# Windowed attention feeding a leaky-ReLU MLP: a new order of the first loads, batch 1 on five banks, and softmax sums over paired halves

## The chip, the cores and the metric

The kernel runs on one core of a Trainium2 chip. The metric is the device time of one execution in microseconds (us), measured around the whole program; the kernel before takes 304.47 us (median of 3 runs, 304.13 to 305.33).

## The reference, cut to what matters

```python
# q, k, v: (8 batches, 8 heads, 576 tokens, 64), float32
scores = q @ k.T / 8
# heads 0-3 (plain):   token i sees j with 0 <= i - j < 32
# heads 4-7 (dilated): token i sees j with 0 <= i - j < 128 and (i - j) % 4 == 0
attn = exp(scores - max) ;  attn /= sum(attn)
x = (attn @ v), heads side by side        # (4608 tokens, 512)
h = x @ w_in                              # w_in (512, 2048)
out = maximum(0.01 * h, h) @ w_out        # w_out (2048, 512), out (4608, 512)
```

## The kernel before, in words

**Attention.** A batch is worked in four *visits* of two heads each, in the order 2, 3, 0, 1: visits 2 and 3 are the dilated heads (group g = 1), visits 0 and 1 the plain ones (g = 0). Keys are cut into nine steps of 64; a visit has two *units* of 288 queries (`unit`, L685). A unit is a chain over all engines: TensorE makes the scores in a PSUM bank (L732), ScalarE takes the exponential into a tile `ee` (L739), VectorE multiplies with a 0/1 mask table (L743, batches 2 to 7; in batches 0 and 1 TensorE adds a bias instead, L728), TensorE sums the exponentials over keys by a matmul with a block of ones (L754, `z`) and multiplies with V (L756, both print as L750), ScalarE turns the sum into its reciprocal by Ln and Exp (L761, L763), and VectorE writes the normalised result as float16 into `xt` (L774). In a plain unit the score matmuls of 96 columns overlap: a query of the second half of a step's 96 columns meets the next step's first 32, so that 416 columns of `ee` fold into 288 sums.

**Getting there.** For batches 2 to 7 the planner's DMAs fetch rows of 128 bytes, GpSimd casts them to float16 (L373), and VectorE transposes 32x32 blocks (L585, L590, L597). Batches 0 and 1 (`EARLY`) are fetched in longer rows: the first 512 tokens of q and k in rows of 1 KB (`load_qk`, L429), the last 64 tokens apart (`load_rest`, L475), and TensorE turns them: four transposes at a time for the long part (`turn`, L620), eight for the last tokens (`turn_rest`, L661), both by way of one bank, `tp`. The turned pieces go on into the operand slots by copies on VectorE and ScalarE (L384, L386). `turn_rest` stands behind the second visit's `turn` (L1074 to L1076). V of the early dilated visits (`load_v` with g = 1, L510 to L516) comes in six DMAs, each into 64 partitions.

**MLP.** Tokens are cut into twelve chunks of 384. `up` (L784) multiplies a chunk with w_in, 16 blocks j of 128 hidden rows, four visits each (L793), and ScalarE applies the leaky ReLU into `gt` (L808). Chunk 1 straddles batches 0 and 1 and is done in two halves of 192 columns with one activation per block and half. Chunks 9 to 11 go through `up_seven` (L1157), a form with seven products instead of eight. The first four token tiles of 128 go through `down` (L820): 16 matmuls of 512 columns with w_out (L832), in parts of four blocks; the other 32 tiles in eight groups of four (`group`, L872, matmuls L922), which also need sums of w_out made by VectorE (L862).

**Order.** Nothing is ordered by hand but the first loads. `FIRST` (L29) lists them: w0 to w7 are w_in in pieces of 0.5 MB, w8 to w15 w_out, `qbg` is q and k of batch b, group g (1.05 MB; `q01` is batch 0, dilated), `rb` the last 64 tokens of batch b (0.26 MB), `vbg` the values (0.59 MB), `c` the mask table (0.4 MB); a dot gives one more place to a value load that comes in pieces. All go to SyncE's DMA queue in that order (two of `q01` and the identity matrix go by ScalarE's). Everything else is a task with engines to choose from, an assumed duration (such as the costs in `cast`, L366, and `move`, L387), a latency and its dependences; `_Plan.forward` (L93) simulates the engines, multiplying durations by `MARGIN` once the planned time is past `CALM` (L22, L27), `backward` gives new priorities, and the best of nine passes fixes the instruction order of every engine. An engine works strictly in that order. Filler matmuls (L1301) fill planned TensorE gaps at the start.

**Banks.** PSUM has eight banks: `tp` for turning, `sps`, `ops` x2 for attention, `hps` x2 for `up`, `fps` x2 for `down`. A bank is passed on in the order in which tasks are created (`grab`, L341). Batch 0 also uses `fps[0]` and `hps[1]` (L1078); batch 1 has three banks (L1080).

Of the kernel before, what the change touches and what calls it, by code (L numbers as in the profile page):

```python
# [18 lines left out]
RAMP = 0  # L19
# [7 lines left out]
def _margin(name, at):  # L27
    return MARGIN[name] if at > CALM else 1.0
FIRST = ('w0 q01 r0 v01 . q00 . . . . w1 v00 . w2 w3 w4 w5 w6 w7 q11 r1 q10 v11 w8 w9 . '  # L29
         'w10 v10 . . . w11 . w12 . w13 . c . w14 w15')  # L30


def _constants():
# [5 lines left out]
    last = []  # L39
# [5 lines left out]
    plain1 = [band] * 3 + [band[:, :64], band[:, 32:]]  # L45
# [204 lines left out]
def kernel(  # L250
# [54 lines left out]
    vst = [sbuf(f"vst{i}", [128, 1152], FP32) for i in range(NVS)]  # L305
    slots = sbuf("slots", [128, NT * TS])
    turned = [sbuf(f"turned{i}", [128, 640]) for i in range(NX)]
    ee = [sbuf(f"ee{i}", [128, 512]) for i in range(NE)]
# [56 lines left out]
    def cast(dst, src, n, deps, prio, engines=("POOL", "DVE"), slow=1.0):  # L365
        cost = {"POOL": (0.05 + n * 0.00102) * slow, "DVE": 0.07 + n * (0.00055 if slow == 1.0 else 0.0011),  # L366
                "ACT": (0.06 + n * 0.00087) * slow}

        def fn(e):
            if e == "ACT":  # L370
                nc.scalar.copy(out=dst, in_=src)
            else:
                ENG[e].tensor_copy(out=dst, in_=src)  # L373
        return add(tuple((e, cost[e]) for e in engines), None, 0.2, deps, fn, prio, 0.0, "cast")
# [5 lines left out]
    def move(dst, src, n, deps, prio, eng=("DVE",), dense=False):  # L380

        def fn(e):
            if e == "ACT":
                nc.scalar.copy(out=dst, in_=src)  # L384
            else:
                ENG[e].tensor_copy(out=dst, in_=src)  # L386
        cost = {"DVE": 0.11 + n * (0.00062 if dense else 0.001), "ACT": 0.08 + n * 0.00095,  # L387
                "POOL": 0.07 + n * 0.0011}
# [100 lines left out]
    def load_v(b, g, prio, at_step=None):  # L489
# [5 lines left out]
        def when(x):  # L495
            n[0] += 1
            return at_step[n[0] - 1] if at_step else prio + x
        for hh in range(2):
# [76 lines left out]
    def turn(b, vi, prio):  # L575
# [5 lines left out]
        if b >= EARLY:  # L581
# [4 lines left out]
            if dil:  # L586
# [4 lines left out]
                q_ready[b, vi] = [add("POOL", 0.72, 0.2, [tq] + old, lambda e: nc.gpsimd.tensor_copy(  # L591
# [63 lines left out]
    def turn_rest(b, prio):  # L655
        c, r_users = raw[b, "rest"]
        t_old, t_users = grab(tpb)

        def pe(e):
            for i in range(8):  # L660
                nc.tensor.transpose(tpb[:, i * 64:i * 64 + 64], rest[0:64, i * 128:i * 128 + 128],  # L661
                                    ident[0:64, 0:64])
        tt = add("PE", 0.23, 0.25, c + [t_id] + t_old, pe, prio, 0.2)
        r_users.append(tt)
        for g in (1, 0):
# [3 lines left out]
            if g:  # L669
                dst = slot(t0, 128, 0, 128, [TS, 2], [144, 4], [1, 16])  # L670
                src = at(tpb, 0, 128, g * 128, [64, 2], [1, 4], [4, 16])
            else:
                dst = slot(t0, 512, 0, 128, [TS, 2], [1, D])
                src = at(tpb, 0, 128, g * 128, [64, 2], [1, D])
            mq = move(dst, src, 128, [tt] + old, prio, ("DVE", "ACT"))
            mk = [move(slot(t0, KB + 1024 + 64 * hh, 64 * hh, 64 * hh + 64, [TS, 2], [1, D]),
                       at(tpb, 64 * hh, 64 * hh + 64, 256 + g * 128, [64, 2], [1, D]), 128,
                       [tt] + old, prio, ("DVE", "ACT")) for hh in range(2)]
# [4 lines left out]
    bank_at = [0]  # L683

    def unit(b, vi, u, prio, banks):  # L685
# [25 lines left out]
        elif u == 0:  # L711
# [3 lines left out]
            bias = [(0, 384, 0, [[0, 4], [1, 96]]), (384, 32, 0, [[1, 32]])]  # L715
        else:
            n = 416
            steps = [(s, [[1, 96]], 64 * s, 96 * (s - 5), 96, 64 * s - 288, [[1, 96]]) for s in (5, 6, 7)]
            steps.append((8, [[1, 64]], 512, 288, 64, 224, [[1, 64]]))
            steps.append((4, [[1, 64]], 288, 352, 64, 0, [[1, 64]]))  # L720
            bias = [(0, 288, 0, [[0, 3], [1, 96]]), (288, 64, 0, [[1, 64]]), (352, 64, 32, [[1, 64]])]
# [32 lines left out]
        t_sum_ = add("PE", 0.188, 0.25, [t_m, t_e, t_id], second(p_bank, lambda s: block_ones),  # L754
                     prio, 0.4, "z")
# [28 lines left out]
    def up(c, j, x, n, batches, acc, ht, by_block):  # L784
# [28 lines left out]
        acc[j].append((t_a, x, n))  # L813

# [57 lines left out]
    def group(four, acts, at_time, split):  # L872
# [33 lines left out]
        def add_up(dst, a, b, op, deps, who, t_late=0.0):  # L906
            t = add("DVE", 0.63 if n_g > 3 else 0.78, 0.2, deps,
# [139 lines left out]
    for i, step in enumerate(steps):  # L1047
        if step[0] == "v":
            rows[step] = [clock[0] + 1 + i]
            waiting += [step] * {"v01": 5, "v11": 5, "v00": 1, "v10": 3}[step]  # L1050
        elif step == ".":
            rows[waiting.pop(0)].append(clock[0] + 1 + i)
# [14 lines left out]
    def attend(b, first, step):  # L1067
# [20 lines left out]
    def ups(c, x, n, batches):  # L1088
        for j in range(NJ):
# [5 lines left out]
    U_SEVEN = (9, 10, 11)  # L1095
    HF, HT = DFF // 2, 192
# [60 lines left out]
    def up_seven(c, j0, batches, ts, acc, banks, when):  # L1157
# [70 lines left out]
        p7 = product(w_sum_of(3), x_sum_of(3), "Z", True, [s_t[3], ts[3][2]], 3)  # L1228
# [15 lines left out]
    def last_seven():  # L1244
# [8 lines left out]
        for order, c in enumerate(U_SEVEN):  # L1253
            batches = [[c // 3 * 2], [c // 3 * 2, c // 3 * 2 + 1], [c // 3 * 2 + 1]][c % 3]
            ts = x_sums(c, batches, order)
            for n in range(4):
                banks = [ready.pop(0) for _ in range(3)]
                up_seven(c, 2 * n, batches, ts, all_acts[c], banks, begins[c] + 2.5 * n)
                ready += before + [banks[1]]
                before = [banks[0], banks[2]]  # L1260

    n_g = 0
    for m in range(B // 2):
# [4 lines left out]
        if 3 * m not in U_SEVEN:  # L1268
            ups(3 * m, 0, 384, [e])
        if m == 0:  # L1270
# [6 lines left out]
        else:  # L1277
            attend(o, WHEN[o], 6.5)
            if 3 * m + 1 not in U_SEVEN:
                ups(3 * m + 1, 0, 384, [e, o])  # L1280
        if 3 * m + 2 not in U_SEVEN:
# [10 lines left out]
        while n_g < len(groups) and all(all_acts[c][0] for c, _ in groups[n_g]):  # L1292
            four = groups[n_g]
            group(four, all_acts, begins[four[-1][0] + 1] + four[-1][1] * 2.0, n_g == len(groups) - 1)
            n_g += 1
# [56 lines left out]
```

## Time and profile before

| | |
|---|---|
| median of 3 runs | 304.47 us (304.13 to 305.33) |
| the profiled execution | 303.41 us |
| its span in the trace | 301.5 us |
| TensorE (PE) busy | 288.6 us, 96% |
| VectorE (DVE) busy | 218.7 us, 73% |
| ScalarE (ACT) busy | 217.1 us, 72% |
| GpSimd (POOL) busy | 136.7 us, 45% |
| moved by DMA | 47.17 MB |

The span runs from the first to the last instruction of the profiled execution; the time around it (1.9 us) is start and end of the program. PE, DVE, ACT and POOL are the engines, SPq the queue of the engine that issues most DMAs. A matmul's row counts from issue to a modelled end, so consecutive matmuls overlap in the records; what one costs is read from start to start. In brackets behind a timeline row stands the engine's idle time before it and what ended it.

### The profile page before, as it was taken

The numbers are of one execution on the slowest core, as the hardware profiler recorded it, in microseconds if no ns is written. First come the engines' busy times: TensorE is split into PE (matmuls) and PEld (weight loads), VectorE is DVE, ScalarE is ACT, GpSimd is POOL, SyncE is SP. The second block draws the span as 40 slices with busy tenths as digits, with TensorE's granted clock in tenths as the row PEclk, the third lists the DMA queues.
The fourth block names the chain that finished last, engine by engine and source line by source line (L and its number), as shares of the span: only waits on it lengthen the run. The fifth ranks groups of instructions, "written<-read, shape, count | busy, mean of one in ns | idle before, by whom it ended". The sixth has DMA issues, their size and how long they took to land.

```text
span 301.5 us, 7912 instructions
## 1 busy us (share of the span) xinstructions
PE 288.6 (96%) x3038; PEld 227.9 (76%) x3038; DVE 218.7 (73%) x386; ACT 217.1 (72%) x509; POOL 136.7 (45%) x194
## 2 busy tenths in 40 slices
PE   5889989899999999999999999999999999999995
PEld 2466666568766789777777777877788999999984
DVE  5586464898568979876747779799964878587832
ACT  1497886568897775799688877688777778868321
POOL 5365434386678948778567984487000000000000
PEclk9999999999999999999999999999999999999999
DMA  7999999979988978997998999771201110011123
GB/s 241 303 339 371 293 275 282 158 152 177 161 176 164 235 160 164 207 163 157 193 167 200 161 219 170 142 183 36 72 2 49 57 37 1 10 65 70 37 104 105
DMA packets 156102, 47.17 MB, mean 156 GB/s; under 512 B 136864, under 2 KB 153376, under 8 KB 156064
## 3 DMA queue, kind: packets, MB, share of 16 engines
q1 hardware_dynamic: 155376, 46.04, 65.8%
q10 hardware_dynamic: 688, 0.63, 0.6%
q8 instruction: 23, 0.38, 0.5%
q14 instruction: 15, 0.12, 0.1%
HBM read 37.22 MB, written 9.44 MB: 155 GB/s over the span
## 4 chain that ended last, share of the span: by engine, by line
PE 81%; DMA 12%; DVE 2%; ACT 2%; SPq 1%; POOL 1%; issue 1%; DVEq 0%; POOLq 0%; ACTq 0%
PE hps L793 26%; PE fps L922 23%; PE tp L922 8%; DMA xt<-in_moe_w_out_dram 5%; DMA stg<-in_q_dram 5%; PE ops L750 4%; PE hps L1185 4%; PE ops L1185 4%; PE fps L832 3%; PE sps L750 2%; DMA vst<-in_v_dram 2%; PE ops L732 2%; PE sps L1185 1%; PE ops L922 1%; PE sps L732 1%; ACT slots L384 1%
## 5 line engine op out<-in xcount | busy, mean ns | idle before, releaser
L793 PE MATMUL hps<-xt,w_in 128*128 128x384 f16 (+1 forms) x616 | 107.4, 309 | 1.2 <-ACT gt L808 0.8
L808 ACT ACTIVATE gt<-hps 128x384 f16<-128x384 f32 (+1 forms) x154 | 69.1, 458 | 21.6 <-PE hps L793 19.8
L922 PEld LDWEIGHTS <-gt 128*128 128x128 f16 x768 | 72.4, 98 | 9.8 <-DVE gt L908 0.3
L793 PEld LDWEIGHTS <-w_in 128*128 128x128 f16 x640 | 56.4, 98 | 26.2 <-issue 1.9
L373 POOL CAST nat<-stg 128x576 f16<-128x576 f32 (+1 forms) x55 | 41.7, 779 | 30.2 <-DMA stg<-in_k_dram 20.7
L373 POOL CAST slots<-vst 64x576 f16<-64x576 f32 x53 | 47.0, 900 | 10.3 <-PE hps L793 4.4
L922 PE MATMUL fps<-w_out,gt 128*128 128x256 f16 x368 | 47.0, 272 | 0.0
L743 DVE TENSOR_TENSOR ee<-ee,con 128x384 f16<-128x384 f16 (+1 forms) x48 | 27.9, 582 | 13.4 <-ACT ee L739 13.1
L763 ACT ACTIVATE rc<-rc 128x288 f32<-128x288 f32 x64 | 27.7, 445 | 1.0
L774 DVE TENSOR_TENSOR xt<-ops,rc 128x288 f16<-128x288 f32 x42 | 18.8, 449 | 11.5 <-ACT rc L763 10.8
L386 POOL COPY slots<-turned 64x64 f16<-64x64 f16 (+2 forms) x41 | 21.6, 531 | 6.3 <-DVE turned L585 1.9
L739 ACT ACTIVATE ee<-ops 128x384 f16<-128x384 f32 (+1 forms) x41 | 20.5, 502 | 5.5 <-PE ops L732 5.5
L750 PEld LDWEIGHTS <-con 128*128 128x128 f16 x320 | 19.1, 98 | 4.8 <-issue 1.0
L732 PEld LDWEIGHTS <-slots 128*128 128x128 f16 x320 | 19.1, 97 | 4.5 <-ACT slots L384 0.2
L951 ACT COPY stg<-fps 128x512 f32<-128x512 f32 (+1 forms) x24 | 12.8, 533 | 11.4 <-PE fps L922 10.2
L750 PEld LDWEIGHTS <-slots 128*128 128x128 f16 x320 | 17.5, 97 | 3.5 <-issue 1.2
L761 ACT ACTIVATE rc<-ops 128x288 f32<-128x288 f32 x41 | 16.7, 411 | 4.1 <-PE ops L750 4.1
L585 DVE STREAM_TRANSPOSE turned<-nat 128x576 f16<-128x576 f16 x24 | 17.9, 760 | 1.3 <-POOL nat L373 1.3
L1212 ACT ACTIVATE gt<-slots 128x384 f16<-128x384 f32 x36 | 17.7, 526 | 1.4 <-DVE slots L1205 1.4
L832 PE MATMUL fps<-w_out,gt 128*128 128x512 f16 x64 | 16.6, 378 | 1.1 <-POOL w_out L373 0.7
L384 ACT COPY slots<-turned 64x576 f16<-64x576 f16 (+1 forms) x24 | 16.0, 666 | 1.1 <-DVE turned L585 0.8
L1185 PEld LDWEIGHTS <-stg 128*128 128x128 f16 x192 | 16.4, 98 | 0.4
(121 smaller groups left out, 504.1 us busy)
## 6 DMA issues: line engine op xcount, KB each, us to landing
out_dram<-osb SPq DMA_DIRECT2D x32, 256.0 KB, 2.6
stg<-in_q_dram SPq DMA_DIRECT2D x48, 144.0 KB, 3.6
stg<-in_k_dram SPq DMA_DIRECT2D x48, 144.0 KB, 3.4
vst<-in_v_dram SPq DMA_DIRECT2D x32, 128.0 KB, 3.1
vst<-in_v_dram SPq DMA_DIRECT2D x14, 288.0 KB, 4.3
gt<-in_moe_w_in_dram SPq DMA_DIRECT2D x6, 512.0 KB, 6.5
stg<-in_q_dram SPq DMA_DIRECT2D x3, 512.0 KB, 7.0
stg<-in_k_dram SPq DMA_DIRECT2D x3, 512.0 KB, 6.5
```

The source lines that it names most:

```text
L373: ENG[e].tensor_copy(out=dst, in_=src)
L386: ENG[e].tensor_copy(out=dst, in_=src)
L732: nc.tensor.matmul(p_bank[:, c:c + w], slot(tn, KB + 128 * s, 0, 128, [1, 128]), slot(tn, qx, 0, 128, *qd), start=first or not by_pe, stop ...
L739: lambda e: nc.scalar.activation(out=et[:, 0:n], in_=p_bank[:, 0:n], func=AF.Exp, scale=SCALE), prio)
L743: lambda e: nc.vector.tensor_tensor(out=et[:, 0:n], in0=et[:, 0:n], in1=con[:, table:table + n], op=ALU.mult), prio,
L750: nc.tensor.matmul(at(dst, 0, 128, o, *od), lhs(s), et[:, c:c + w], start=i == 0, stop=i == len(steps) - 1, skip_group_check=True)
L763: lambda e: nc.scalar.activation(out=rt, in_=rt, func=AF.Exp, scale=-1.0), prio)
L793: nc.tensor.matmul(ht[:, 0:n], at(w_in, 0, 128, vi * DFF + j // 2 * 256 + j % 2, [2, 128]), at(xt[m % 2], 0, 128, vi * 1152 + x0 + x, [1, n]),
L808: lambda e: nc.scalar.activation(out=gt[c % NG][:, j * n_c + x:j * n_c + x + n], in_=ht[:, 0:n], func=AF.Prelu, alpha=0.01),
L832: nc.tensor.matmul(ft, g[:, j * n_c + tt * 128:j * n_c + tt * 128 + 128], w_out[:, j * DM:j * DM + DM], start=(j == 0), stop=(j == NJ - 1))
L922: nc.tensor.matmul(bk[:, x:x + HN], tl[:, off + j * step:off + j * step + 128], rhs(j), start=first and x == 0 and j == 0, stop=j == HJ - ...
L1185: nc.tensor.matmul(b[:, i * HT:i * HT + HT], lhs(v, j0 + i), rhs(v), start=first and i == 0 and v == 0, stop=i == 1 and v == 1, skip_group ...
```

## The change

It has nine parts.

1. `FIRST` is reordered: r0 comes first, w0 moves behind q00, w8 to w10 come ahead of all of batch 1, w11 to w13 ahead of q10 and v10, and c goes last.
2. `turn_rest` turns in two lots of four. For batch 0 it stands ahead of all visits and uses the bank `hps[1]`; for batch 1 it stands ahead of the second visit.
3. Early dilated values come in two DMAs (one of 128 partitions, one for the last tokens) instead of six, and are cast in ten pieces instead of four.
4. Batch 1's attention gets `hps` as well: five banks.
5. In batches 2 to 7 a plain unit's `ee` gets 128 more columns: DVE or POOL adds the overlapping parts there, and the `z` matmuls take 288 columns in three (u = 0) or two (u = 1) instead of 416 in five. Column order of u = 1 changes to suit.
6. Chunk 1's halves go through `up_pair`: two blocks in one bank and one activation for both.
7. The first two of chunk 9's `up_seven` rounds use only the two `hps` banks, with one bank for both Y and Z.
8. Groups are created as soon as their chunks are (`down_groups`), not at the end of a pair of batches.
9. The planner's assumed costs: POOL's casts and copies get a larger constant, `MARGIN` falls (ACT 1.045 to 1.02, DVE 1.154 to 1.062, POOL 1.018 to 1.0), `CALM` 49.7 to 38.8.

```diff
-MARGIN = {'ACT': 1.045, 'DVE': 1.154, 'POOL': 1.018, 'PE': 1.0, 'SP': 1.0, 'DMA': 1.133, 'LAND': 1.15}
-CALM = 49.7
+MARGIN = {'ACT': 1.02, 'DVE': 1.062, 'POOL': 1.0, 'PE': 1.0, 'SP': 1.0, 'DMA': 1.133, 'LAND': 1.15}
+CALM = 38.8
...
-FIRST = ('w0 q01 r0 v01 . q00 . . . . w1 v00 . w2 w3 w4 w5 w6 w7 q11 r1 q10 v11 w8 w9 . '
-         'w10 v10 . . . w11 . w12 . w13 . c . w14 w15')
+FIRST = ('r0 q01 v01 . q00 w0 v00 . w1 w2 w3 w4 w5 w6 w7 w8 w9 w10 q11 w11 r1 v11 . w12 '
+         'w13 q10 v10 w14 . w15 . . c')
...
-        cost = {"POOL": (0.05 + n * 0.00102) * slow, "DVE": ...
+        cost = {"POOL": 0.15 + n * 0.00102 * slow, "DVE": ...
...
-                "POOL": 0.07 + n * 0.0011}
+                "POOL": 0.24 + n * 0.001}
...
+        if g == 1 and b < EARLY:
+            t_main = load("SP", at(vs, 0, 128, 0, [256, 4], [1, 256]),
+                          dram(v, base, [4 * D, 128], [HS, 4], [1, 256]), 512, 1024, v_old, when(0.0))
+            t_last = load("SP", at(vs, 0, 64, 1024, [D, 4], [1, D]),
+                          dram(v, base + 512 * D, [D, 64], [HS, 4], [1, D]), 256, 256, v_old, when(0.01))
+            t0 = slot_of[b, 2]
...
+            last = [cast(slot(t0, VB + hh + 1024, 64 * hh, 64 * hh + 64, [TS, 2], [2, D]),
+                         at(vs, 0, 64, 1024 + 128 * hh, [D, 2], [1, D]), 128,
+                         [t_last] + old[0] + old[1], prio, ("POOL", "DVE", "ACT"), 1.3) for hh in range(2)]
+            v_users += last
+            for j in range(2):
+                made = [cast(slot(t0 + j, VB + hh + 512 * i, 64 * hh, 64 * hh + 64, [128, 4], [2, D]),
+                             at(vs, 64 * i, 64 * i + 64, (2 * hh + j) * 256, [D, 4], [1, D]), 256,
+                             [t_main] + old[j], prio, ("POOL", "DVE", "ACT"), 1.3)
+                        for i in range(2) for hh in range(2)]
+                v_users += made
+                v_in[b, 2 + j] = made + last
+            return
...
-        t_old, t_users = grab(tpb)
-
-        def pe(e):
-            for i in range(8):
-                nc.tensor.transpose(tpb[:, i * 64:i * 64 + 64], ...
-        tt = add("PE", 0.23, 0.25, c + [t_id] + t_old, pe, prio, 0.2)
-        r_users.append(tt)
+        t_old, t_users = grab(hps[1] if b == 0 else tpb)
+        bk = hps[1].bitcast(FP16) if b == 0 else tpb
+        tts = []
+        for g in (1, 0):
+            def pe(e, g=g):
+                for i in (2 * g, 2 * g + 1, 2 * g + 4, 2 * g + 5):
+                    nc.tensor.transpose(bk[:, i * 64:i * 64 + 64], rest[0:64, i * 128:i * 128 + 128],
+                                        ident[0:64, 0:64])
+            tts.append(add("PE", 0.115, 0.25, [c[1 - g], c[3 - g], t_id] + t_old, pe, prio, 0.2))
+        r_users += tts
...
+    PLUS, PLUS_FROM = 448, 2
...
+            both = 64, 96
+            sums_of = [(0, [[1, 64]], 0, [[1, 64]]), (128, [[96, 3], [1, 32]], 96, [[64, 3], [1, 32]]),
+                       (PLUS, [[32, 4], [1, 32]], 64, [[64, 4], [1, 32]])]
...
+            both = 32, 64
+            sums_of = [(0, [[96, 5], [1, 32]], 0, [[64, 5], [1, 32]]),
+                       (PLUS, [[32, 4], [1, 32]], 32, [[64, 4], [1, 32]])]
...
-        t_sum_ = add("PE", 0.188, 0.25, [t_m, t_e, t_id], second(p_bank, lambda s: block_ones),
-                     prio, 0.4, "z")
+        if b < PLUS_FROM or dil:
+            t_sum_ = add("PE", 0.188, 0.25, [t_m, t_e, t_id], second(p_bank, lambda s: block_ones),
+                         prio, 0.4, "z")
+        else:
+            def fn(e, x=both[0], y=both[1]):
+                ENG[e].tensor_tensor(out=at(et, 0, 128, PLUS, [32, 4], [1, 32]),
+                                     in0=at(et, 0, 128, x, [96, 4], [1, 32]),
+                                     in1=at(et, 0, 128, y, [96, 4], [1, 32]), op=ALU.add)
+            t_both = add((("DVE", 0.3), ("POOL", 0.55)), None, 0.2,
+                         [t_m, t_e], fn, prio, 0.0, "m")
+
+            def add_over(e):
+                for i, (x, dx, o, od) in enumerate(sums_of):
+                    nc.tensor.matmul(at(p_bank, 0, 128, o, *od), block_ones, at(et, 0, 128, x, *dx),
+                                     start=i == 0, stop=i == len(sums_of) - 1, skip_group_check=True)
+            t_sum_ = add("PE", 0.13, 0.25, [t_m, t_e, t_id, t_both], add_over, prio, 0.4, "z")
...
+    def up_pair(c, j, x, n, batches, acc, ht):
+        m, x0, n_c = chunks[c]
+        h_old, h_users = grab(ht)
+
+        def pe(e):
+            for k in range(2):
+                for i, vi in enumerate(VISITS):
+                    nc.tensor.matmul(ht[:, k * n:k * n + n],
+                                     at(w_in, 0, 128, vi * DFF + j // 2 * 256 + k, [2, 128]),
+                                     at(xt[m % 2], 0, 128, vi * 1152 + x0 + x, [1, n]),
+                                     start=k == 0 and i == 0, stop=k == 1 and i == NI - 1,
+                                     skip_group_check=True)
...
+        t_a = add("ACT", 0.06 + 2 * n * 0.00085, 0.22, [t_p] + gt_free.get(c - NG, []),
+                  lambda e: nc.scalar.activation(
+                      out=at(gt[c % NG], 0, 128, j * n_c + x, [n_c, 2], [1, n]), in_=ht[:, 0:2 * n],
+                      func=AF.Prelu, alpha=0.01),
+                  begins[c] + j * 1.3 - 5)
...
         for n, vi in enumerate(VISITS):
+            if b < EARLY and n == b:
+                turn_rest(b, first + step * n)
             turn(b, vi, first + step * n)
-            if b < EARLY and n == 1:
-                turn_rest(b, first + step * n)
...
-            banks = dict.fromkeys(VISITS, three)
+            banks = dict.fromkeys(VISITS, three + hps if b == 1 else three)
...
+        if n == 192:
+            pool = hps
+            for j in range(0, NJ, 2):
+                up_pair(c, j, x, n, batches, all_acts[c], pool[j // 2 % len(pool)])
+            return
...
-                banks = [ready.pop(0) for _ in range(3)]
+                if c == 9 and n < TWO:
+                    banks = [hps[n % 2], hps[1 - n % 2], hps[1 - n % 2]]
+                else:
+                    banks = [ready.pop(0) for _ in range(3)]
+                    ready += before + [banks[1]]
+                    before = [banks[0], banks[2]]
                 up_seven(c, 2 * n, batches, ts, all_acts[c], banks, begins[c] + 2.5 * n)
...
+            down_groups()
```

More of the change, by code (lines that the diff above doesn't have):

```diff
@@ L1049 @@
             rows[step] = [clock[0] + 1 + i]
-            waiting += [step] * {"v01": 5, "v11": 5, "v00": 1, "v10": 3}[step]
+            waiting += [step] * {"v01": 1, "v11": 1, "v00": 1, "v10": 3}[step]
         elif step == ".":
@@ L1095 @@
     U_SEVEN = (9, 10, 11)
+    TWO = 2
     HF, HT = DFF // 2, 192
@@ L1291 @@
             part_free[0] = part_free[1] = rings["STG"][-1]
[L1292 to L1295, printed above, removed]
+        down_groups()
     order = plan.run()
```

60 lines of the change are left out of this document (38 added, 22 removed).

## The prediction

> **What bounds the kernel now.** First the page's busy line and the stretches view (us, then busy time and count of PE, PEld, DVE, ACT, POOL, then clock, DMA share, GB/s).
>
> ```profile
> PE 288.6 (96%) x3038; PEld 227.9 (76%) x3038; DVE 218.7 (73%) x386; ACT 217.1 (72%) x509; POOL 136.7 (45%) x194
> ...
> 0.00:20.00 20.00, 14.22 (x130) 8.10 (x131) 12.65 (x27) 9.17 (x20) 10.97 (x22) 1.00 1.00 282
> 20.00:40.00 20.00, 19.25 (x217) 13.87 (x216) 11.99 (x29) 16.59 (x44) 8.96 (x15) 1.00 1.01 332
> 40.00:59.00 19.00, 16.28 (x182) 11.00 (x179) 12.11 (x22) 12.64 (x35) 6.73 (x9) 1.00 1.03 239
> 59.00:299.00 240.00, 238.82 (x2517) 194.89 (x2515) 181.91 (x310) 178.67 (x414) 110.06 (x149) 1.00 0.59 126
> ```
>
> There are two regimes. From 59 to 299 us PE is busy 238.82 of 240 us: only less PE work, or an earlier start of this full stretch, moves the end. Before 59 us the DMA share is 1.00 to 1.03: the first loads are the limit, and PE has holes. Next the chain of waits (start, us, what), to see which load the full stretch waits for.
>
> ```profile
> 19.36 9.68 DMA stg<-in_q_dram
> ...
> 31.46 7.10 DMA xt<-in_moe_w_out_dram
> 38.57 6.42 DMA vst<-in_v_dram
> ...
> 46.77 8.89 DMA xt<-in_moe_w_out_dram
> 55.72 0.88 POOL w_out L373
> ```
>
> It runs from load to load. The last link is w15, the end of w_out: issued at 46.77, landed at 55.66, cast by 56.6, and the `down` matmuls that lacked it go on. Full use of PE begins there.
>
> **The change part by part.** Prices on PE first, from start to start in the timeline.
>
> ```profile
> 30.68 1.46 PE L793 MATMUL hps<-xt,w_in 128*128 128x384 f16 x8
> 31.98 0.39 PE L620 MATMUL tp<-con,nat 128*128 128x128 f16 x4
> ...
> 59.04 1.02 PE L832 MATMUL fps<-w_out,gt 128*128 128x512 f16 x4
> 59.90 0.35 PE L750 MATMUL ops<-ee,con 128*128 128x96 f16 x5
> ...
> 87.45 0.35 PE L750 MATMUL ops<-ee,con 128*128 128x96 f16 x5
> 87.65 0.81 PE L793 MATMUL hps<-xt,w_in 128*128 128x384 f16 x4
> ```
>
> An `up` matmul of 384 columns costs 1.30/8 = 0.163 us (0.42 ns a column), a `down` matmul of 512 columns 0.86/4 = 0.215, a plain unit's five `z` matmuls of 416 columns 0.20.
>
> *Start of batch 0 (r0 first and in its own bank, v01 in two loads, w0 later).* From the timelines of DVE, PE, ACT and POOL:
>
> ```profile
> 8.99 0.43 DVE L386 COPY slots<-fps 64x512 f16<-64x512 f16 x1
> ...
> 12.60 0.29 PE L661 MATMUL tp<-con,rest 64*128 64x64 f16 x4 [0.64 <-DVE rest L373]
> ...
> 14.29 0.50 ACT L739 ACTIVATE ee<-sps 128x384 f16<-128x384 f32 x1
> ...
> 14.91 0.89 POOL L373 CAST slots<-vst 64x576 f16<-64x576 f32 x1 [0.32 <-DMA vst<-in_v_dram]
> ...
> 20.26 0.32 PE L793 MATMUL hps<-xt,w_in 128*128 128x384 f16 x1
> ```
>
> Visit 2's long part is in its slots at 9.4, but the last tokens are turned only at 12.6 and hold the first exponential until 14.29. With r0 at the head of the queue they come before the long part, and the scores can start near 9.5. r0 takes the place of w0 (0.26 for 0.52 MB), and v01 stands ahead of q00, 1 MB sooner. So the first `up` should come near 15.5 instead of 20.26, once w0 has landed. v01's ten casts in place of four go to engines that have 7 to 11 of these 20 us free. What PE gains by 28 us follows from the count of L793 (stretches of that line: us, PE busy and count):
>
> ```profile
> 0.00:28.00 28.00, 5.01 (x25) 1.00 1.01 315
> 28.00:40.00 12.00, 9.36 (x63) 1.00 0.99 289
> 40.00:56.60 16.60, 4.81 (x44) 1.00 1.06 253
> ```
>
> Today 25 of chunk 0's 64 are issued by 28 us. With batch 0 finished by then, the 32 of the first eight blocks and some 6 of the next two can be; the others need w7, whose place in the queue (7.8 MB) does not move. The lead at 28 us is 13 x 0.163 = 2.1 us.
>
> *w_out ahead of most of batch 1.* Does the lead last? With the DMA share at 1, landings go by volume. The two ends, w7 and w15, and the stretch of `down`'s line L832 up to w15:
>
> ```profile
> 27.48 0.64 POOL L373 CAST w_in<-wst 128x512 f16<-128x512 f32 x1 [0.58 <-DMA wst<-in_moe_w_in_dram]
> ...
> 55.72 0.87 POOL L373 CAST w_out<-xt 128x512 f16<-128x512 f32 x1 [1.50 <-DMA xt<-in_moe_w_out_dram]
> ...
> 40.00:56.60 16.60, 7.07 (x26) 1.00 1.06 253
> ```
>
> From 27.4 to 55.7 us go 8.14 MB, 0.288 MB/us. In the new order that puts (estimates from this rate) w10 at 32.9, q11 at 36.5, v11 at 41.3, w13 at 44.9, q10 at 48.5, v10 at 50.6, w14 at 52.4, w15 at 54.2 and c at 55.7 us. By the same rate q10 is at 35.6 today: it moves back 13 us. w15 moves up 1.5 us, because c (0.41 MB) goes behind it. Now what PE can have done when w15 is cast. Today, at 56.6: chunks 0 and 1a, 26 of 64 `down` matmuls, and batch 1 but for its last units. In the new order, at 55.0: the same chunks, at most 24 `down` matmuls (two banks, three parts of four each that need no w14 and w15), and about as much of batch 1. It is the same work. So the lead of 2.1 us runs dry between 39 and 55 us, where PE again waits for loads, and what is left is that the full stretch begins 56.6 - 55.0 = **1.6 us** earlier. The bounds: -4 (batch 1 too late, below) and +3.7 (the lead kept on top).
>
> *Two-load values, five banks and pairs.* No PE work goes. SyncE issues eight DMAs fewer, on a queue that the DMA engines hold up: 0. ACT saves 32 x 0.335 - 16 x 0.490 = 2.9 us:
>
> ```profile
> L808 ACT ACTIVATE gt<-hps 128x192 f16<-128x192 f32 x32 | 10.0, 335 | 4.0 <-PE hps L793 4.0
> L808 ACT ACTIVATE gt<-hps 128x384 f16<-128x384 f32 x122 | 59.2, 490 | 17.6 <-PE hps L793 15.8
> ```
>
> But there ACT waits for PE (4.0 us), and it has 6 of the 19 us up to 59 free: 0.
>
> *Paired halves.* Batches 2 to 7 have 24 plain units. 288 columns at 0.42 ns and the issue are 0.135 us, against 0.20: 24 x 0.065 = **1.5 us** less on the bound engine (between 0 and 24 x 0.12 = 2.9, if it went by matmul count). Added are 24 additions of 128 columns on DVE or POOL, which the trace does not have. The nearest rows:
>
> ```profile
> L743 DVE TENSOR_TENSOR ee<-ee,con 128x416 f16<-128x416 f16 x24 | 14.4, 601 | 6.6 <-ACT ee L739 6.4
> ...
> L386 DVE COPY slots<-tp 64x128 f16<-64x128 f16 x5 | 1.1, 223 | 2.1 <-ACT slots L384 2.1
> ...
> 92.09 0.34 DVE L743 TENSOR_TENSOR ee<-ee,con 128x384 f16<-128x384 f16 x1
> ...
> 200.00:220.00 20.00, 20.00 (x212) 15.38 (x210) 19.41 (x33) 15.93 (x36) 8.90 (x11) 1.00 0.19 62
> ```
>
> From 0.22 (a small copy) to 0.60 (the mask product's mean); I take 0.34, the quickest product of the same kind. That is 8.2 us on engines that have 58 (DVE) and 130 us (POOL) free after 59 us. The new wait stands ahead of `z` on PE; behind it queue `up` matmuls such as those at 87.65, and ACT waits for both. As long as the planner puts enough PE work ahead of `z`, it costs 0; without that cover 24 x 0.34 = 8 us.
>
> *Chunk 9 on two banks, groups created earlier, new assumed costs.* No work goes or comes. With Y and Z in one bank, PE waits for one more DVE operation in two rounds (at most 2 x 0.60 = 1.2 us, covered while `down` work is at hand). Assumed DVE times fall by 8% (1.062 for 1.154), so PE is packed closer behind DVE; 58 us of free DVE time speak for 0, the stretch from 200 to 220 us against it (below).
>
> **Sum:** 1.6 + 1.5 = 3.1 us. The profiled execution took 303.41 us (span 301.5, 1.9 around it), so 300.3; the runs' median lies 1.06 above that execution: **301.4 us**.
>
> **The rivals.** *The lead is kept* (298.0). If the first loads take less time than today's rate says, PE does not run dry before 55 us. For it:
>
> ```profile
> 5.00:10.00 5.00, 4.06 (x18) 1.63 (x16) 2.63 (x7) 0.98 (x2) 1.30 (x3) 1.00 1.11 279
> ...
> 20.00:25.00 5.00, 4.81 (x74) 3.75 (x73) 4.60 (x10) 4.58 (x13) 1.84 (x4) 1.00 1.02 406
> ```
>
> DMA moves 279 GB/s among r0 and the values, loads of 64 partitions, and 406 among the 128-partition weight pieces. v01 and v11 (1.18 MB) at 406 instead of 279 take 1.3 us less; with the 2.1 us lead that is 3.4 below the forecast. Against it: r0 and v00 stay as they are, and 4 KB rows may explain the 406. [...]
>
> *DVE takes the place of the loads* (304.5, no change). From 200 to 220 us DVE is busy 19.41 of 20 us. Batches 6 and 7 add 8 x 0.34 = 2.7 us there, and the planner now counts on a quicker DVE; if 0.4 us more comes out of waiting, the 3.1 us are spent. Against: POOL has 11 of these 20 us free, and PE had no hole there. The spread of the product, 0.34 to a mean of 0.60, shows that it is held up by something. [...]
>
> *Batch 1 comes too late* (308.4, slower). `down` has 40 matmuls left at 55.0 us: 8.6 us, until 63.6. Then chunk 1b needs all of batch 1, whose q10 lands at 48.5. It decides whether q10's chain takes more than 15 us. Batch 0's took 15.5 from the landing of q00, batch 1's took 10 from its last values, with three banks:
>
> ```profile
> 11.79 0.61 POOL L373 CAST nat<-stg 128x512 f16<-128x512 f32 x1 [1.99 <-DMA stg<-in_q_dram]
> 26.86 0.46 DVE L774 TENSOR_TENSOR xt<-hps,rc 128x288 f16<-128x288 f32 x1 [0.42 <-ACT rc L763]
> ...
> 52.56 0.49 DVE L373 CAST slots<-vst 64x576 f16<-64x576 f32 x1 [2.50 <-DMA vst<-in_v_dram]
> ...
> 61.36 0.89 DVE L774 TENSOR_TENSOR xt<-ops,rc 128x288 f16<-128x288 f32 x2
> ```
>
> From v10 at 50.6 the 10 us end at 60.6, in time; from q10 15.5 us end at 64.0, nearly. If the turning through the one bank `tp` and eight units of chain stretch it to 22 us, PE stands still from 63.6 to 70.5, since group 0 needs chunk 1b too: 301.4 + 7 = 308.4.
>
> **How the numbers follow.** Forecast 301.4 (own range 299.4 to 302.9): 0.52. Lead kept, 298.0: 0.15. DVE, 304.5: 0.17. Batch 1 late, 308.4: 0.16. The range 297.0 to 305.8 leaves out the last. 0.5%, about what a measurement of this kernel can tell from no change, is 1.5 us: faster means below 302.95, slower above 306.0. Faster takes the first two, 0.67; same 0.17; slower 0.16.
>
> **What would show it.** Right: the first exponential near 10 us, the first L793 near 15.5; 38 of L793 by 28 us; holes on PE between 39 and 55 us, and none after the last cast of w_out near 55; `z` of a plain unit at 0.13 to 0.14 from start to start. Wrong: PE holes after 60 us with VectorE or ScalarE as releaser, a last cast of w_out later than 56, the last L774 of batch 1 later than 64.

## The result and the profile after

The changed kernel takes **299.51 us** (median of 6 runs, 298.23 to 301.25), the kernel before on the same chip 304.3 us (6 runs): a ratio of **0.985 [0.981, 0.990]**, 4.5 us less. One run of before, at 309.07 us, was in a slower state and is left out of the ratio. The forecast was 301.4 with a range of 297.0 to 305.8. The profiled execution took 299.23 us, with a span of 297.3 (before 303.41 and 301.5).

The busy line of the page after:

```profile
PE 285.0 (96%) x2975; PEld 226.4 (76%) x2975; DVE 221.7 (75%) x406; ACT 218.9 (74%) x502; POOL 142.7 (48%) x201
```

And the stretches (us, then busy time and count of PE, PEld, DVE, ACT, POOL, clock, DMA share, GB/s):

```profile
0.00:20.00 20.00, 14.35 (x153) 9.50 (x154) 14.81 (x32) 11.38 (x26) 11.32 (x25) 0.91 0.91 278
20.00:40.00 20.00, 18.31 (x176) 12.67 (x175) 10.57 (x27) 13.99 (x33) 9.40 (x13) 1.00 1.05 374
40.00:59.00 19.00, 18.90 (x233) 13.21 (x232) 15.24 (x29) 14.96 (x38) 7.18 (x13) 1.00 1.01 226
59.00:300.00 241.00, 233.41 (x2420) 191.00 (x2418) 181.11 (x320) 178.59 (x408) 114.80 (x153) 1.00 0.58 124
```

From 40 to 59 us PE is busy 18.90 of 19 us, where it was 16.28; the hole-free stretch now begins near 30 us. The last row is the one to compute with: at 59 us PE has 233.41 us of work left, where it had 238.82. That is 5.4 us less: 24 paired units at 0.07 are 1.7 of it, and the rest, 3.7 us, is put down to work done earlier. The counts of `down`'s matmuls behind 59 us (before, then after) bear this out, for 16 of them at 0.215 are 3.4 us:

```profile
L832 PE MATMUL fps<-w_out,gt 128*128 128x512 f16 x32 | 7.9, 378 | 0.0
L902 PE MATMUL fps<-w_out,gt 128*128 128x512 f16 x16 | 3.8, 380 | 0.0
```

Against it stands PE's idle time behind 59 us, which is the span less 59 less that work: 297.3 - 59 - 233.4 = 4.9 us, where it was 301.5 - 59 - 238.8 = 3.7. So the span's 4.2 us are **3.7 from the start + 1.7 from the halves - 1.2 in new idle time**. Of the idle time 3.2 us lie behind the last matmul (before 3.6), so some 1.7 us are holes, where before had 0.1. The chain of waits after names the same end of the first loads as before:

```profile
30.46 8.89 DMA vst<-in_v_dram
...
41.02 9.40 DMA xt<-in_moe_w_out_dram
50.47 0.88 POOL w_out L373
```

w15 landed at 50.42, not at 55.66. The new holes behind 59 us, from PE's waits (before has none in this view; what, us in total, times, longest):

```profile
PE ops L761 <- DVE xt L817: 0.7, 1, 0.7
PE ops L779 <- ACT rc L804: 0.6, 1, 0.6
PE sps L761 <- DVE xt L817: 0.2, 1, 0.2
```

The lines after: L761 scores, L768 exponential, L772 mask product, L779 bank of `z` and V, L788 the addition, L796 paired `z`, L804 and L806 Ln and Exp, L817 the normalised result, L836 and L865 `up`, L851 and L877 its activations, L902 `down`, L978 and L992 groups. In these three PE waits for banks that VectorE and ScalarE empty, not for an addition.

### The profile page after: what moved, and what is told of

Same layout as the page of the kernel before. It is cut to its first block, busy times and chain, and to the rows that moved or that the text cites. A ratio compares the mean times of both kernels' runs of the same rounds, so it can differ in the third digit from the quotient of the medians.

```text
span 297.3 us, 7789 instructions
## 1 busy us (share of the span) xinstructions
PE 285.0 (96%) x2975; PEld 226.4 (76%) x2975; DVE 221.7 (75%) x406; ACT 218.9 (74%) x502; POOL 142.7 (48%) x201
## 4 chain that ended last, share of the span: by engine, by line
PE 79%; DMA 8%; DVE 6%; ACT 3%; issue 2%; POOL 1%; SPq 0%; DVEq 0%; POOLq 0%
PE hps L836 22%; PE fps L992 22%; PE tp L992 8%; PE hps L1261 5%; PE ops L1261 3%; DMA xt<-in_moe_w_out_dram 3%; PE ops L779 3%; DMA vst<-in_v_dram 3%; PE fps L902 3%; PE ops L761 2%; PE hps L865 2%; DMA stg<-in_k_dram 2%; PE sps L779 2%; ACT gt L851 1%; DVE slots L386 1%
## 5 line engine op out<-in xcount | busy, mean ns | idle before, releaser
L836 PE MATMUL hps<-xt,w_in 128*128 128x384 f16 x488 | 95.1, 326 | 0.8 <-ACT gt L851 0.8
L992 PEld LDWEIGHTS <-gt 128*128 128x128 f16 x768 | 72.5, 98 | 9.5
L851 ACT ACTIVATE gt<-hps 128x384 f16<-128x384 f32 x122 | 59.1, 491 | 20.0 <-PE hps L836 18.8
L836 PEld LDWEIGHTS <-w_in 128*128 128x128 f16 x512 | 45.9, 98 | 23.2 <-issue 1.2
L373 POOL CAST slots<-vst 64x576 f16<-64x576 f32 (+2 forms) x60 | 54.4, 920 | 7.6 <-DVE slots L386 2.9
L992 PE MATMUL fps<-w_out,gt 128*128 128x256 f16 x368 | 47.0, 273 | 0.0
L373 POOL CAST nat<-stg 128x576 f16<-128x576 f32 (+1 forms) x55 | 40.6, 761 | 12.1 <-DVE xt L817 6.1
L772 DVE TENSOR_TENSOR ee<-ee,con 128x384 f16<-128x384 f16 (+1 forms) x48 | 23.7, 495 | 15.0 <-ACT ee L768 14.8
L806 ACT ACTIVATE rc<-rc 128x288 f32<-128x288 f32 x64 | 27.9, 442 | 0.9
L817 DVE TENSOR_TENSOR xt<-ops,rc 128x288 f16<-128x288 f32 x40 | 18.0, 450 | 12.7 <-ACT rc L806 8.3
L386 POOL COPY slots<-turned 64x64 f16<-64x64 f16 (+2 forms) x36 | 18.6, 525 | 15.1 <-DVE turned L605 7.5
L761 PEld LDWEIGHTS <-slots 128*128 128x128 f16 x320 | 18.7, 99 | 6.5 <-issue 1.4
L788 POOL TENSOR_TENSOR ee<-ee 128x128 f16<-128x128 f16 x9 | 5.3, 586 | 33.9 <-DVE ee L772 29.0
L779 PEld LDWEIGHTS <-slots 128*128 128x128 f16 x320 | 17.8, 97 | 4.7 <-POOL w_in L373 1.0
L768 ACT ACTIVATE ee<-ops 128x384 f16<-128x384 f32 (+1 forms) x39 | 19.5, 504 | 2.2 <-PE ops L761 1.8
L804 ACT ACTIVATE rc<-ops 128x288 f32<-128x288 f32 x39 | 15.8, 408 | 6.0 <-PE ops L796 3.1
L384 ACT COPY slots<-turned 64x512 f16<-64x512 f16 (+1 forms) x28 | 18.6, 663 | 1.9 <-DVE turned L605 1.5
L978 DVE TENSOR_TENSOR gt<-gt 128x1024 f16<-128x1024 f16 x21 | 17.2, 821 | 0.2 <-PE fps L992 0.2
```

Of the source, the lines that this page charges most:

```text
L761: nc.tensor.matmul(p_bank[:, c:c + w], slot(tn, KB + 128 * s, 0, 128, [1, 128]), slot(tn, qx, 0, 128, *qd), start=first or not by_pe, stop ...
L768: lambda e: nc.scalar.activation(out=et[:, 0:n], in_=p_bank[:, 0:n], func=AF.Exp, scale=SCALE), prio)
L772: lambda e: nc.vector.tensor_tensor(out=et[:, 0:n], in0=et[:, 0:n], in1=con[:, table:table + n], op=ALU.mult), prio,
L779: nc.tensor.matmul(at(dst, 0, 128, o, *od), lhs(s), et[:, c:c + w], start=i == 0, stop=i == len(steps) - 1, skip_group_check=True)
L806: lambda e: nc.scalar.activation(out=rt, in_=rt, func=AF.Exp, scale=-1.0), prio)
L836: nc.tensor.matmul(ht[:, 0:n], at(w_in, 0, 128, vi * DFF + j // 2 * 256 + j % 2, [2, 128]), at(xt[m % 2], 0, 128, vi * 1152 + x0 + x, [1, n]),
```

## The experiments

Two theories stood against each other. **Start and halves:** the loads reach PE sooner and `z` is cheaper, as forecast. **Plan:** any edit makes the planner order all engines anew, and the order itself is worth several us, whatever the edit. Each ratio is to the kernel before on the same chip; on the chips used its medians are 303.9 to 304.3 us. The changed kernel was not run again with the later sets; f6, measured beside n1 and n2 and two loads away from it, shows with its 0.988 that the gain is still there. The table adds, from the profiled execution, the start of w15's cast, PE's work left at 59 us and its idle time behind 59 us.

| kernel | median us | ratio to before | w15 cast | work left | idle behind |
|---|---|---|---|---|---|
| before | 304.3 | 1 | 55.7 | 238.8 | 3.7 |
| changed | 299.51 | 0.985 [0.981, 0.990] | 50.5 | 233.4 | 4.9 |
| *planned anew* | | | | | |
| e1 no halves | 304.61 | 1.003 [0.999, 1.006] | 52.7 | 237.6 | 5.9 |
| e2 old order of loads | 303.31 | 1.002 [0.998, 1.005] | 53.7 | 235.7 | 6.7 |
| e3 six loads | 308.31 | 1.017 [1.014, 1.021] | 54.1 | 239.6 | 8.0 |
| e4 mask table sooner | 304.63 | 1.005 [1.003, 1.008] | 53.1 | 235.8 | 8.1 |
| n1 margin nudged | 304.73 | 1.002 [1.000, 1.005] | 52.9 | 238.2 | 7.7 |
| n2 calm nudged | 303.77 | 0.999 [0.996, 1.002] | 50.5 | 235.8 | 6.8 |
| *order kept* | | | | | |
| f1 no halves | 301.87 | 0.992 [0.989, 0.995] | 51.5 | 235.8 | 5.1 |
| f2 six narrow loads | 303.59 | 0.999 [0.996, 1.002] | 55.5 | 238.4 | 5.1 |
| f5 six loads, four wide | 303.25 | 0.996 [0.993, 0.999] | 56.3 | 239.3 | 5.1 |
| f6 three loads | 300.52 | 0.988 [0.984, 0.991] | 49.9 | 233.2 | 5.1 |
| f3 mask table sooner | 302.50 | 0.995 [0.992, 0.998] | 55.0 | 238.1 | 4.8 |
| f4 before, with halves | 303.69 | 0.998 [0.995, 1.002] | 56.9 | 239.7 | 4.3 |

The profiled executions of f5 and n1 lie 2 us above their medians, those of f3 and f4 1.1 to 1.3 above, that of f6 1.4 below: their last columns are too high or too low by a part of that.

**Parts undone, planned anew.** Four single edits of the changed kernel (e3 goes back to before's way of fetching the early dilated values, and so to its four casts too):

```diff
-    PLUS, PLUS_FROM = 448, 2                     # e1
+    PLUS, PLUS_FROM = 448, 8
-FIRST = ('r0 q01 v01 . q00 w0 ...')              # e2: before's order, values in two loads
+FIRST = ('w0 q01 r0 v01 . q00 w1 v00 . ...')
-        if g == 1 and b < EARLY:                 # e3
+        if False:
-          'w13 q10 v10 w14 . w15 . . c')         # e4
+          'w13 q10 v10 c . . . w14 w15')
```

> The changed kernel without paired halves (every plain unit sums 416 columns in five matmuls). Theory (the halves take 24 x 0.07 us off a full TensorE): 1.7 us more than the changed kernel, ratio to the kernel before near 0.991. Rival (the added operation and its wait cause the new holes of 0.6 us at 84 us and 0.9 us at 202 to 207 us, so the halves bring nothing net): the holes are gone too, and the ratio stays near 0.985.

> The changed kernel with the old order of the first loads (values still in two loads). Theory (the end is set by when the last of w_out lands, 5.2 us sooner in the changed kernel): the last of w_out is cast near 55 us again, TensorE has holes of some 3 us between 40 and 57 us, and 3 to 4 of the 4.4 us are lost: ratio 0.995 to 0.998. Rival (the gain comes from batch 0's early start and from the planner's new costs): at most 1.5 us are lost, ratio below 0.990.

> The changed kernel with the early dilated values in six loads of 64 partitions, as before, at the same place of the queue. Theory (the two wide loads are why DMA moved 0.32 instead of 0.29 MB/us between 27 and 50 us): GB/s between 30 and 45 us falls from 350 to some 300, the last of w_out lands near 52.5 instead of 50.4 us, time up by 1.5 to 2 us, ratio 0.990 to 0.992. Rival (the rate comes from what is behind w_out now, the mask table and half of batch 1's plain values): same landing within 0.5 us, ratio 0.984 to 0.987.

> The changed kernel with the mask table and all of batch 1's plain values ahead of the last two pieces of w_out (0.7 MB). Theory (the full stretch begins when the last of w_out is cast): it lands 2.2 us later, near 52.6 us, TensorE gets holes of 1.5 to 2.2 us around 52 us, and the time rises by as much: ratio 0.990 to 0.993. Rival (TensorE has other work at hand, so that this landing has slack): no holes, time the same, ratio near 0.985.

All four lose the whole gain or more, outside everything that was expected of them: 4.9 to 9.7 us above the changed kernel (differences of ratios by 304.3 us). If the parts simply added up, that could not be, since together they gained 4.5. The last two columns say where it goes. The work left at 59 us is 2.3 to 6.2 us above the changed kernel's, for e1 too (4.2, of which 1.7 can be the halves), whose edit touches nothing ahead of 59 us. And PE idles 5.9 to 8.1 us behind 59 us, against 4.9, each time at another place. The longest such wait of e1, and that of e2:

```profile
PE fps L992 <- DVE gt L978: 1.3, 1, 1.3
```

```profile
PE sps L761 <- POOL slots L611: 1.9, 1, 1.9
```

So these four could not price a part: the edit and a new order of 7,800 instructions are mixed in them. What followed split the two.

**The plan alone.** Two kernels with the changed kernel's work, in which only a constant of the planner moves:

```diff
-MARGIN = {'ACT': 1.02, 'DVE': 1.062, ...         # n1
+MARGIN = {'ACT': 1.02, 'DVE': 1.064, ...
-CALM = 38.8                                      # n2
+CALM = 38.0
```

> The changed kernel with one of the planner's constants moved by two thousandths (VectorE's margin 1.062 to 1.064): no work is added or taken away, every queue's order is planned anew. Theory C, the order that the planner happened on is itself worth several us, and what an undone part showed when everything was planned anew was mostly that: a ratio to before of 0.995 to 1.010, with holes of 1 us or more on PE behind 60 us as in those runs. Rival: orders planned from the same costs are alike, a ratio of 0.980 to 0.990.

> As the run before, by another constant: the moment from which the planner's margins count, 38.8 to 38.0 us. Theory C: a ratio to before of 0.995 to 1.010, and holes on PE behind 60 us at other places than in the changed kernel. Rival: 0.980 to 0.990.

Both are back at the time of before: 5.2 and 4.1 us lost (each +-1.7) with no work added or taken away. n1's waits on PE from 60 to 220 us:

```profile
PE ops L761 <- DVE xt L817: 1.5, 1, 1.5
PE hps L836 <- ACT gt L851: 0.8, 2, 0.5
PE hps L865 <- ACT gt L877: 0.8, 1, 0.8
PE tp L992 <- DVE gt L978: 0.5, 1, 0.5
```

In n2, PE is idle for 2.1 us from 80 to 100 us alone, in three waits:

```profile
80.00:100.00 20.00, 17.92 (x174) 12.42 (x173) 17.50 (x33) 16.64 (x39) 12.86 (x17) 1.00 0.95 195
```

n2 has the early w15 (50.5) and its work left is still 2.4 us above the changed kernel's; n1 lags by 4.8 there. A new order thus costs in both places, the start and the holes. The theory of the plan holds: of the 4.5 us, about all hang on this one order. It does not rule out the other theory; what the parts are worth within one order is the next question.

**Parts undone, order kept.** In these runs every engine has the instruction order of the changed kernel (f4: of the kernel before), and one thing differs. First the halves:

```diff
-            def fn(e, x=both[0], y=both[1]):     # f1: no addition,
-                ENG[e].tensor_tensor(...)
+            def fn(e):
+                pass
...
-            t_sum_ = add("PE", 0.13, 0.25, [t_m, t_e, t_id, t_both], add_over, prio, 0.4, "z")
+            t_sum_ = add("PE", 0.13, 0.25, [t_m, t_e, t_id, t_both],
+                         second(p_bank, lambda s: block_ones), prio, 0.4, "z")
```

> The changed kernel with every engine's order of instructions kept as it is, only the 24 additions left out and the full five sum matmuls put in their place. Theory (the paired halves are worth 24 x 0.07 us; the other 3.6 us that the re-planned kernel without them lost came from its other instruction order): 1.7 us more than the changed kernel, less what the vanished waits give back, ratio to the kernel before 0.988 to 0.991. Rival (the halves themselves are worth the whole 5 us): ratio near 1.003.

Undoing them costs 2.0 us (+-1.7). The work left rises by 2.4, of which w15's cast, 1.1 us later, may be a part; the idle time does not fall without the additions (5.1 for 4.9). So the halves are a gain of PE work, and their new wait costs nothing that can be seen in this order. In before's order they were tried too:

```diff
+        def mask():                              # f4: before.py with the new columns of ee
+            nc.vector.tensor_tensor(...)         # the mask product, and right behind it on DVE
+            if halves:
+                nc.vector.tensor_tensor(...)     # the addition
...
-        t_sum_ = add("PE", 0.188, ..., second(p_bank, lambda s: block_ones), ...)
+        t_sum_ = add("PE", 0.188, ..., add_over if halves else second(...), ...)
```

> The kernel before, its engines' order kept, only with paired halves: VectorE adds right behind the mask product of a plain unit, and the sums take 288 columns in three or two matmuls. Theory (they save TensorE 24 x 0.07 us, and the additions lie beside its work): 1.7 us less than the kernel before, ratio 0.993 to 0.996. Rival (the additions delay the chain on VectorE by as much as they save): ratio 0.998 to 1.002.

0.998 [0.995, 1.002] lies in the rival's range, and its interval just reaches into the theory's: it can't be told from no change. In its profiled execution the halves do take work off PE (busy 286.2 us on its page, 288.6 before), but ahead of 59 us PE is idle 3.2 us longer (busy 16.45 us from 20 to 40 us, against 19.25). The edit changes only a column order in batches 0 and 1; why the start is worse is not known, so this run leaves the size open.

Next, how soon w15 lands. f3 puts the mask table and the three last pieces of v10 ahead of w14 and w15 on SyncE's queue:

```diff
+    moved = v_late + [t_con[0]]                  # f3
+    order = [t for t in order if t not in moved]
+    x = order.index(w_load[14])
+    order[x:x] = moved
```

> The changed kernel, engines' order kept, only the mask table and the last three pieces of batch 1's plain values moved ahead of the last two pieces of w_out in SyncE's queue (0.7 MB). Theory (the full stretch of TensorE begins when the last of w_out is cast): it lands 2.2 us later, near 52.6 us, TensorE stands still for about that long near 52 us, ratio 0.990 to 0.993. Rival (this landing has slack): no new hole, ratio 0.984 to 0.987.

w15's cast moves from 50.5 to 55.0, and PE now waits for it. The cast:

```profile
54.98 0.87 POOL L373 CAST w_out<-xt 128x512 f16<-128x512 f32 x1 [1.52 <-DMA xt<-in_moe_w_out_dram]
```

And PE's wait:

```profile
PE fps L904 <- DVE w_out L373: 2.5, 2, 2.3
```

That costs 2.8 us (+-1.7): six tenths of the delay, so the landing had some slack. What stands behind w15 in the queue is therefore a large part of the change. By volume it was to land 2.2 us later, and it was 4.5. SyncE reaches v10's pieces 1.1 us later than in the changed kernel, which the edit does not explain, and is then held for 8.4 us by the five loads ahead of w14:

```profile
38.74 6.75 SPq L358 DMA_DIRECT2D vst<-in_v_dram  x4
45.53 1.67 SPq L358 DMA_DIRECT2D con<-consts  x1
```


Last, the values in two loads, which the forecast had priced at 0. Three ways to load the same bytes:

```diff
+            def main(e):                         # f2: four loads of 64 partitions, 2 heads
+                for i in range(2):
+                    for j in range(2):
+                        nc.sync.dma_start(at(vs, 64 * i, 64 * i + 64, 512 * j, ...), ...)
+            def main(e):                         # f5: four loads of 128 partitions, 1 head
+                for j in range(4):
+                    nc.sync.dma_start(at(vs, 0, 128, 256 * j, [1, 256]), ...)
+            def final(e):                        # f2 and f5: the last tokens in two
...
+            def main(e):                         # f6: two loads of 64 partitions, 4 heads
+                for i in range(2):
+                    nc.sync.dma_start(at(vs, 64 * i, 64 * i + 64, 0, [256, 4], [1, 256]), ...)
```

> The changed kernel, engines' order kept, only the early dilated values fetched by six loads of 64 partitions at the same place of the queue. Theory (loads over half the partitions slow DMA down): GB/s between 30 and 45 us falls below 320, the last of w_out lands 1.5 us or more later than 50.4, ratio 0.990 to 0.993. Rival (the number of loads and their width do not matter, the 9.7 us that the re-planned kernel lost came from its order): landing within 0.5 us, ratio 0.984 to 0.987.

> Order of every engine kept as in the changed kernel; the early dilated values come by six loads again, but the four large ones take 128 partitions and one head each (128 lines of 1 KB, as each of the narrow ones had). Theory A, the number of loads on SyncE is what costs (each 0.6 to 1.9 us of SyncE's issue there, and the ones behind them wait): as slow as the six narrow loads, a ratio to before of 0.996 to 1.002, a last w_out cast near 55 us, 30 to 45 us near 280 GB/s. Theory B, the width of 64 partitions costs: as fast as the changed kernel, a ratio of 0.982 to 0.989, the cast near 50.5 us, 350 GB/s.

> Order kept; the large load of the early dilated values is cut in two of 64 partitions by four heads (256 lines of 1 KB each), the last tokens stay one load: one DMA more in each of batches 0 and 1, and the width of before. Theory A (number of loads): nearly the changed kernel, a ratio of 0.983 to 0.990, the last w_out cast near 51 us. Theory B (width of 64 partitions): as slow as the six narrow loads, a ratio of 0.995 to 1.002, the cast near 55 us.

f2 loses 4.2 us and f5 3.2, f6 only 0.7 (each +-1.8). Wide or narrow makes no difference that can be measured; the number of loads does (f2 and f6 are both narrow, and f2 is 3.4 us +-1.5 slower). f2 and f5 have eight loads more than the changed kernel over the two batches, 0.46 us each on average; f6 has two, for which the same price gives 0.9. SyncE's queue shows where it goes (start, us, what, count). The changed kernel from v11 to the next load, w11:

```profile
30.46 3.04 SPq L358 DMA_DIRECT2D vst<-in_v_dram  x2
33.60 0.54 SPq L358 DMA_DIRECT2D gt<-in_moe_w_out_dram  x1
```

The same loads in f2:

```profile
31.90 4.62 SPq L507 DMA_DIRECT2D vst<-in_v_dram  x4
36.77 2.50 SPq L512 DMA_DIRECT2D vst<-in_v_dram  x2
41.26 0.33 SPq L358 DMA_DIRECT2D gt<-in_moe_w_out_dram  x1
```

In f5:

```profile
32.52 4.23 SPq L506 DMA_DIRECT2D vst<-in_v_dram  x4
37.10 1.87 SPq L511 DMA_DIRECT2D vst<-in_v_dram  x2
40.15 0.33 SPq L358 DMA_DIRECT2D gt<-in_moe_w_out_dram  x1
```

And in f6:

```profile
28.82 2.00 SPq L506 DMA_DIRECT2D vst<-in_v_dram  x2
30.87 0.66 SPq L358 DMA_DIRECT2D vst<-in_v_dram  x1
32.05 0.33 SPq L358 DMA_DIRECT2D gt<-in_moe_w_out_dram  x1
```

Two or three loads keep w11's load back for 3.1 to 3.2 us, six for 9.4 in f2 and 7.6 in f5. The loads' own rows are 2.7 to 3.0 us of it, and 7.1 and 6.1 with six; the rest is mostly SyncE's wait ahead of w11 until an earlier load of w_out has landed (1.9 us in f2, 1.1 in f5). Meanwhile the DMA engines run short. The stretch of 30 to 45 us, first the changed kernel, then f2, then f6 (f5 lies between, with a DMA share of 0.97 and 307 GB/s):

```profile
30.00:45.00 15.00, 15.00 (x148) 10.92 (x148) 8.64 (x22) 9.92 (x24) 7.75 (x12) 1.00 1.10 351
```

```profile
30.00:45.00 15.00, 12.47 (x94) 8.17 (x94) 6.92 (x20) 7.82 (x20) 7.82 (x12) 0.93 0.94 277
```

```profile
30.00:45.00 15.00, 15.00 (x156) 11.28 (x155) 8.37 (x22) 10.32 (x25) 7.57 (x12) 1.00 1.11 329
```

f6's pairs of 64-partition loads lose 0.7 us +-1.8 to one load of 128, and f5's wide loads gain nothing on f2's narrow ones that can be measured (0.9 us +-1.4), so the partitions are not what the two loads mainly gained by. Why one issue of a small load takes SyncE over a microsecond there (4.62 us for four) was not tried apart; the trace names the landing of earlier loads as what it waits for in part of that time (1.0 us at these four, 1.3 us at the two behind them).

## Why the prediction was right, point by point

The direction held, and so did the kind of both causes: an earlier start, and less PE work for `z`. The size was short by 1.9 us: 299.5 for 301.4, just inside the forecast's own range and a little nearer to the rival *the lead is kept* (298.0). Of the 1.9 us, 1.1 are in the profiled execution (299.23 for 300.3), and 0.8 because the median after lies only 0.3 above that execution, not 1.06. In the span 1.6 + 1.5 were forecast, and 3.7 + 1.7 - 1.2 came: two errors of opposite sign, a start priced too low and holes priced at 0, so that the number lies as near as it does is in part luck. Of its signs of being right, `z` at 0.13 us came, the first exponential came 1.1 us late, and the other three did not come; of its signs of being wrong, one came, PE holes after 60 us with VectorE and ScalarE as releasers. By its steps:

- **The full stretch begins 1.6 us earlier: mis-sized, 3.7.** Two terms failed. "SyncE issues eight DMAs fewer, on a queue that the DMA engines hold up: 0" is worth 3 to 4 us by f2 and f5 in the changed kernel's order, for the queue was held up by its issues too. And the volumes ahead of w15 were listed wrongly: only two of v10's four pieces stand ahead of it, so 0.29 MB more than c stand behind. Together they brought w15 down at 50.4 where 54.2 was forecast. From 27.1 to 50.4 us the loads ran at some 0.32 MB/us (7.4 MB by the landings, an estimate), not at the 0.288 that was carried over from before.
- **The lead of 2.1 us runs dry between 39 and 55 us: wrong.** No hole over 0.3 us lies between 31 and 60 us, and 27 `down` matmuls are issued by 51.37, where at most 24 were to be by 55.0. The rival *the lead is kept* (298.0) described this part, by faster loads; the reason it gave, width, is not borne out by f5 and f6.
- **First `up` near 15.5, 38 of L793 by 28 us: too early.** The first exponential came at 11.14 (forecast near 10, before 14.29), the first `up` at 19.12, and 34 of that line were issued by 28 us (timeline, then the stretch of L836):

```profile
11.14 0.49 ACT L768 ACTIVATE ee<-sps 128x384 f16<-128x384 f32 x1
...
12.76 2.13 POOL L373 CAST slots<-vst 64x128 f16<-64x128 f32 x4 [2.91 <-DVE slots L386]
...
15.51 1.36 POOL L373 CAST w_in<-gt 128x512 f16<-128x512 f32 x2
...
18.32 0.36 PE L761 MATMUL sps<-slots 128*128 128x96 f16 x5 [0.53 <-DVE slots L386]
...
19.12 0.33 PE L836 MATMUL hps<-xt,w_in 128*128 128x384 f16 x1
```

```profile
0.00:28.00 28.00, 5.99 (x34) 3.21 (x35) 0.94 0.94 315
```

  POOL waits 2.91 us for VectorE ahead of four small casts of v01, and w0's cast queues behind them: the ten casts in place of four, costed at nothing for the engines' free time, have a place in a queue. That is not all of it, for w0 is cast by 16.87, and the first `up` then stands in PE's order behind scores that wait for VectorE's copies into the slots. Which of the two costs more was not tried.
- **Paired halves 24 x 0.065 = 1.5: right.** Start to start a paired `z` takes 0.13 (three matmuls) or 0.12 (two), as here, and f1 measures 2.0 +-1.7:

```profile
104.77 0.29 PE L796 MATMUL ops<-ee,con 128*128 128x64 f16 x3
104.90 0.81 PE L836 MATMUL hps<-xt,w_in 128*128 128x384 f16 x4
...
107.27 0.29 PE L796 MATMUL ops<-ee,con 128*128 128x160 f16 x2
107.39 0.35 PE L779 MATMUL ops<-ee,slots 128*128 128x64 f16 x5
```

- **The addition 0.34 us, its wait 0: the wait right, the price low on average.**

```profile
L788 DVE TENSOR_TENSOR ee<-ee 128x128 f16<-128x128 f16 x15 | 6.2, 412 | 0.3
L788 POOL TENSOR_TENSOR ee<-ee 128x128 f16<-128x128 f16 x9 | 5.3, 586 | 33.9 <-DVE ee L772 29.0 <-DMA stg<-in_k_dram 4.9
```

  0.41 on VectorE and 0.59 on GpSimd on average (the medians are 0.22 and 0.43), inside 0.22 to 0.60, and f1's holes are no smaller without them. The rival *DVE takes the place* did not come about through them.
- **New assumed costs, no hole behind 60 us: wrong by 1.2 us.** Holes of the predicted kind, with VectorE and ScalarE as releasers, are there, also in f1; they make 1.6 us, of which a shorter end behind the last matmul gives 0.4 back.
- **Batch 1 too late: did not happen.** Its last L817 starts at 59.77 (before: 61.36), under the 64 that was set.
- **What no step had: the order itself.** "No work goes or comes" was said of new assumed costs and of tasks created earlier, and so they got 0 and no rival. n1 and n2 show that a plan of the same work can be 4 to 5 us slower, as much as the whole gain. The prediction came out right for the plan that was on hand, which is luck as far as its steps go: from them the same 301.4 would have been said of n1 (304.7) and n2 (303.8).

What stays open: whether the nine parts bring anything over many plans. What f1 to f6 price holds for one order, which was planned for the parts as they are; a part that is undone in it may cost more than in an order of its own, and in before's order the halves brought nothing that could be told. Of seven plans with the new kernel's code or nearly that (changed, e1 to e4, n1, n2), the changed one is the fastest, and the other six lie at 303.3 to 308.3; no such sample of the old code's plans was taken.

## What to carry to other kernels

When a planner orders the instructions, price its noise first: move one constant a little (here by 0.2% and by 2%) and see what the time does. An experiment that undoes a part must keep the order of every engine, or it measures the order as well. And count the loads, not only their bytes, where the issuing queue is on the path: in this order a load saved was worth some 0.46 us.

## What was not expected of the hardware

The granted clock of TensorE fell to 0.66 from 10 to 15 us in the changed kernel's profiled execution, and stayed at 1.00 in f6's, which has the same order:

```profile
10.00:15.00 5.00, 4.72 (x71) 4.34 (x71) 3.48 (x10) 4.46 (x13) 2.06 (x5) 0.66 1.11 317
```

```profile
10.00:15.00 5.00, 4.61 (x75) 4.27 (x73) 3.52 (x11) 4.50 (x11) 2.15 (x5) 1.00 1.14 352
```

It cost nothing that can be seen: the spans are 297.3 and 297.2 us, and why it did not show is left open.
